# Part of the output-projection weights gathered onto 112 partitions, and the rows of o laid out to match

## The chip, the cores and the metric

The kernel runs on one core of one Trainium2 chip, with nothing beside it. Its engines are TensorE (PE; PEld is its weight load), VectorE (DVE), ScalarE (ACT), GpSimd (POOL) and SyncE (SP), and it has 16 DMA engines that fill its on-chip memory of 128 partitions from HBM. The metric is the time of one execution on the device in microseconds (us), the median of several runs. The profile is of one further execution. Its span goes from the first to the last instruction.

## The reference

One decode step, in float32: attention with a cached K and V behind a layer norm, then a two-layer perceptron behind another, both with a residual.

```python
B, Sq, D = 2, 1, 512
H, Sk, Dh = 32, 8192, 128
...
q = (x @ wq).reshape(B, Sq, H, Dh).transpose(0, 2, 1, 3)      # x behind a layer norm
scores = jnp.einsum("bhqd,bhkd->bhqk", q, k_cache) * (Dh ** -0.5)
p = softmax(scores, axis=-1)
o = jnp.einsum("bhqk,bhkd->bhqd", p, v_cache)
a = o.transpose(0, 2, 1, 3).reshape(B, Sq, H * Dh) @ wo        # wo: 4096 x 512
...
h = x + a
h2 = h + gelu(layernorm(h) @ w1 + b1) @ w2 + b2                # w1: 512 x 1792
```

K and V are 268 MB each; wq and wo have 8.4 MB each, w1 and w2 3.7 MB each.

## The kernel before

It streams K and V once. The loop runs over 64 pairs `i` of a head `h` and a batch row `b`. A pair's K is one load of 4 MB into a tile of 128 partitions x 32 KB, with 64 keys to a partition (L150 to L152), and so is its V. All of these tiles come from one pool, `kv`, of five buffers; wq before the loop, and w1 and w2 behind it, use the same pool. SP issues all these loads in the order of the program: K of pair i+1, then V of pair i-1, and it waits at each until the tile's last reader is done.

For each half of K (`c` is 0 or 1), VectorE multiplies it by q (L161), and VectorE (L170) and ScalarE (L166) sum over the head's 128 columns. The largest score of a head goes through TensorE (L180, L186), ScalarE takes the exponentials (L194), and two pairs later TensorE multiplies them with V (`values`, L215). `gather` (L222) copies that sum from PSUM. Its 32 filled rows are parts of the sum, sixteen for each batch row; `head_sum` (L232) adds them up with four products, and `head_out` scales them by the inverse of the softmax's sum (L242), so that o of the two batch rows lies in two partitions.

The projection by wo is done in groups of WG = 4 heads, so long as a head is below LG * WG = 28. `load_wo` (L55) loads a group's 512 rows of wo as four rows to a partition, 8 KB in one run, into a tile `wog` from the pool `wts` of two buffers. `head_out` writes o of the group's heads into one tile `orow` of 512 columns; `turn` (L248) transposes every fourth column into PSUM, four times, `turned` copies this to `ot4` (L252) and multiplies its four slices with the four rows (L254), which adds to `rowacc`. Heads 28 to 31 go another way: their wo has a head's 128 rows on the 128 partitions (one load for the four, L58), their o is kept on 128 partitions too, and `project` (L257) adds head by head; the last head is merged with what follows. A tile `late` for this end shares the buffers of `wog` (L338).

The group of wo is loaded at the fourth pair of its own heads, by SP, between a K load and a V load. `behind` orders what an engine does next behind a given instruction. Instruction order on an engine is otherwise that of the program, with small shifts by the scheduler. POOL does nothing but a few memsets and the identity matrix at the start.

At the end, V's last load comes in three pieces, w1 in four and w2 in six, each piece with a completion of its own. ScalarE's queue loads x at the start (L49); b1 and b2 are four small loads (L281, L282) near pair 56.

Of the kernel before, what the change touches and what calls it, by code (L numbers as in the profile page):

```python
# [8 lines left out]

F32 = mybir.dt.float32  # L10
BF16 = mybir.dt.bfloat16
AF = mybir.ActivationFunctionType
ALU = mybir.AluOpType
AX = mybir.AxisListType

P = 128
EPS = 1e-5
QG = 2
WG = 4
CH = 32  # L20
NACT = 10
BUFS = 5
# [5 lines left out]
def tile_decode_block(ctx: ExitStack, tc: tile.TileContext, x, k, v, wq, wo, w1, b1, w2, b2, out):  # L28
    nc = tc.nc
    B, H, SK, DH = k.shape  # L30
    D = x.shape[-1]
# [6 lines left out]
    SCALE = DH ** -0.5  # L38

    const = ctx.enter_context(tc.tile_pool(name="const", bufs=1))  # L40
    wts = ctx.enter_context(tc.tile_pool(name="wts", bufs=2))
    kv = ctx.enter_context(tc.tile_pool(name="kv", bufs=BUFS))
    work = ctx.enter_context(tc.tile_pool(name="work", bufs=3))
    psq = ctx.enter_context(tc.tile_pool(name="psq", bufs=2, space=bass.MemoryType.PSUM))
    psm = ctx.enter_context(tc.tile_pool(name="psm", bufs=3, space=bass.MemoryType.PSUM))
    psa = ctx.enter_context(tc.tile_pool(name="psa", bufs=1, space=bass.MemoryType.PSUM))

    x2 = const.tile([B, D], F32, name="x2")
    nc.scalar.dma_start(x2, x.rearrange("b s d -> (b s) d"))  # L49

    wo_g = {}

    LG = H // WG - 1

    def load_wo(g):  # L55
        t = wts.tile([P, WG, D], F32, name="wog")
        rows = wo[g * WG * DH:(g + 1) * WG * DH, :]
        nc.sync.dma_start(t, rows.rearrange("(h p) n -> p h n" if g == LG else "(p h) n -> p h n", p=P))  # L58
        wo_g[g] = t

    wqv = wq.rearrange("(p r) n -> p r n", r=DC)
# [1 line left out]
    for r in range(0, DC, 2):  # L63
        t = kv.tile([P, 2, H * DH], F32, name="wqs", tag="kv")
        nc.sync.dma_start(t, wqv[:, r:r + 2, :])  # L65
        wqs += [t[:, 0, :], t[:, 1, :]]

    ident = const.tile([P, P], F32, name="ident")
    make_identity(nc, ident)
    epst = const.tile([P, 1], F32, name="epst")  # L70
    nc.vector.memset(epst, EPS)
    eps2 = const.tile([P, 1], F32, name="eps2")
    nc.vector.memset(eps2, EPS * EPS)
    wb = const.tile([P, D], BF16, name="wb")
    nc.vector.memset(wb, 0.0)
# [45 lines left out]
    for r in range(DC):  # L121
        for j in range(QW // 512):
            for n in range(NG):
                nc.tensor.matmul(so2[j][32 * n:32 * n + B], yT[:, r, :],  # L124
                                 wqs[r][:, n * QW + j * 512:n * QW + (j + 1) * 512],
                                 start=(r == 0), stop=(r == DC - 1))
# [16 lines left out]
    rowacc = psa.tile([B, D], F32, name="rowacc")  # L143
    pairs = [(h, b) for h in range(H) for b in range(B)]
    NP = len(pairs)
    ST, MX, MT, GM, LT, RL, SS, OP, OT, OR, TP = {}, {}, {}, {}, {}, {}, {}, {}, {}, {}, {}

    def load(src, i, parts):
        h, b = pairs[i]
        t = kv.tile([P, NS, DH], F32, name="kv", tag="kv")  # L150
        for s0, n in parts:
            nc.sync.dma_start(t[:, s0:s0 + n], src[b, h].rearrange("(p j) d -> p j d", j=NS)[:, s0:s0 + n])  # L152
        return t
# [9 lines left out]
    def by_act(i, c, kt):  # L163
        s = ST[i]
        for j in range((c + 1) * CH - NACT, (c + 1) * CH):
            nc.scalar.activation(kt[:, j, :], kt[:, j, :], AF.Copy, accum_out=s[:, j:j + 1])  # L166
# [28 lines left out]
                                 AF.Exp, bias=nb[:, b:b + 1], scale=SCALE, accum_out=LT[h][:, b:b + 1])  # L195

    def total(h):
        if h >= LG * WG:
            RL[h] = psm.tile([P, B], F32, name="sm")
            nc.tensor.matmul(RL[h], ones, LT[h], start=True, stop=True)  # L200
        else:
            RL[h] = psm.tile([B, 1], F32, name="sm")
            nc.tensor.matmul(RL[h], LT[h], ones[:, 0:1], start=True, stop=True)  # L203

    def inverse(h):
        rl = work.tile(list(RL[h].shape), F32, name="rl" if h >= LG * WG else "rlr")
        nc.vector.reciprocal(rl, RL[h])
        RL[h] = rl

# [13 lines left out]

    def head_sum(h):
        ss = SS.pop(h)
        OP[h] = psm.tile([P, B] if h >= LG * WG else [B, DH], F32, name="sm")
        for j in range(4):
            sj = ss[:, j * DH:(j + 1) * DH]
            if h >= LG * WG:
                nc.tensor.matmul(OP[h], sj, sel[:, :, j], start=(j == 0), stop=(j == 3))  # L230
            else:
                nc.tensor.matmul(OP[h], sel[:, :, j], sj, start=(j == 0), stop=(j == 3))  # L232

    def head_out(h):
        if h >= LG * WG:
            OT[h] = work.tile([P, B], F32, name="ot")
            nc.vector.tensor_tensor(OT[h], OP.pop(h), RL.pop(h), op=ALU.mult)  # L237
        else:
            g, n = divmod(h, WG)
            if n == 0:  # L240
                OR[g] = work.tile([B, WG * DH], F32, name="orow", bufs=2)
            nc.vector.tensor_scalar(OR[g][:, n * DH:(n + 1) * DH], OP.pop(h), RL.pop(h), None, op0=ALU.mult)  # L242

    def turn(g):
        TP[g] = psm.tile([P, WG, B], F32, name="sm")
        o = OR.pop(g).rearrange("b (p r) -> b r p", r=WG)
        for r in range(WG):
            nc.tensor.transpose(TP[g][:, r, :], o[:, r, :], ident[:B, :B])  # L248

    def turned(g):  # L250
        t = work.tile([P, WG, B], F32, name="ot4")
        nc.vector.tensor_copy(t, TP.pop(g))  # L252
        for r in range(WG):
            nc.tensor.matmul(rowacc, t[:, r, :], wo_g[g][:, r, :], start=(g == 0 and r == 0), stop=False)  # L254

    def project(h):
        nc.tensor.matmul(rowacc, OT.pop(h), wo_g[LG][:, h % WG, :], start=False, stop=(h == H - 2))  # L257

    def behind(m):
        return tc.issue_after(m.ins) if m is not None else nullcontext()  # L260
# [4 lines left out]
    for i in range(NP):  # L265
        h, b = pairs[i]
        for c in range(NC):
            if c == 0:
                if i + 1 < NP:
                    kt[i + 1] = load(k, i + 1, whole if i + 1 < NP - 1 else halves)  # L270
                if i % (WG * B) == 3:
                    g = i // (WG * B)
                    if g <= LG - 1:
                        load_wo(g)
                if i == NP - 10:
                    load_wo(LG)
                if i >= 1:
                    vt[i - 1] = load(v, i - 1, whole if i < NP - 1 else halves)
                if i == NP - 8:
                    for e in range(B):  # L280
                        nc.sync.dma_start(b1r[e::32], b1.rearrange("(n f) -> n f", n=NG))  # L281
                        nc.sync.dma_start(b2s[e:e + 1], b2[None, :])  # L282
            with behind(multiply(i, c, kt[i])):
                if b == 0 and c == 0:
                    if h >= 2:
                        head_sum(h - 2)
                        head_out(h - 2)
                    if h >= 1:
                        all_max(h - 1)
                if b == 0 and c == 1 and h >= 1:  # L290
                    inverse(h - 1)
                    if h >= 2 and h % WG == 1 and h < H - 1:
                        turned(h // WG - 1)
            by_act(i, c, kt[i])
            if b == 0 and c == 0 and h >= 1:
                exps(h - 1)
            by_dve(i, c, kt[i])
            if b == 0 and c == 0:
                if h >= 1:
                    total(h - 1)  # L300
                if h >= 2 and (h - 2) // WG == LG:
                    project(h - 2)
                elif h >= 2 and (h - 2) % WG == WG - 1:
                    turn((h - 2) // WG)
            if c == 1:
                if i >= 2:
                    values(i - 2, vt.pop(i - 2))
                    if b == B - 1:
                        gather(h - 1)
                row_max(i)  # L310
                if b == 0 and h % QG == 1 and h + 1 < H:
                    make_q(h + 1)
# [10 lines left out]
    hl = H - 1  # L323
# [6 lines left out]
    inverse(hl)  # L330
    junk = const.tile([P, 2], F32, name="junk")
    nc.scalar.activation(junk[:, 0:1], LT[hl][:, 0:1], AF.Sqrt)
    wl = wo_g[LG][:, hl % WG, :]
    wsum = const.tile([P, 1], F32, name="wsum")
    nc.vector.tensor_reduce(wsum, wl, axis=AX.X, op=ALU.add)
    wmean = const.tile([P, 1], F32, name="wmean")
# [4 lines left out]
    base = late[:B, 1, :]  # L341
# [17 lines left out]
    last = values(NP - 1, vlast)  # L359
    gather(hl)  # L360
    with behind(last):
        for n in range(NG):
            last = nc.tensor.matmul(po2[32 * n:32 * n + 32], ident[:B, :32], resb[:, n * P:(n + 1) * P],
                                    start=True, stop=False)
# [10 lines left out]
    for c in range(DC):  # L375
        last = nc.tensor.matmul(acc[:, c, :], wlc.rearrange("d (p c) -> d c p", c=DC)[:, c, :], OT[hl],
                                start=True, stop=True)
    with behind(last):
        for n in range(NG):
            nc.tensor.matmul(po2[32 * n:32 * n + B], OT[hl], wl[:, n * P:(n + 1) * P],  # L380
                             start=False, stop=False)
# [8 lines left out]
    for c in range(DC):  # L390
        for n in range(NG):
            last = nc.tensor.matmul(
                pf[32 * n:32 * n + B], cen[:, c, :], w1t[:, c, n * FN:(n + 1) * FN],
                start=(c == 0), stop=(c == DC - 1))
        if c == 0:
            with behind(last):
                for n in range(NG):
                    last = nc.tensor.matmul(vp[32 * n:32 * n + 32], sv, onesd, start=True, stop=True)
# [14 lines left out]
    for t in range(FT):  # L413
        for n in range(NG):
            nc.tensor.matmul(po2[32 * n:32 * n + B], fT[:, t, :B], w2t[:, t, n * P:(n + 1) * P],
                             start=False, stop=(t == FT - 1))
# [29 lines left out]
```

## Time and profile before

| what | value |
|---|---|
| median of 3 runs | 1324.13 us (1324.02 to 1324.27) |
| the profiled execution | 1324.32 us |
| its span | 1322.5 us |
| VectorE busy | 989.5 us, 75% |
| TensorE busy | 530.4 us, 40% |
| ScalarE busy | 442.0 us, 33% |
| POOL busy | 1.3 us, 10 instructions |
| DMA | 561.64 MB, 425 GB/s over the span |
| mean granted TensorE clock | 0.664 |

A line of a group of instructions reads: source line, engine, operation, output and input tiles, shapes, count, then the busy time in us and the mean ns of one, then the idle time of the engine before them and what ended it. The stretch view gives for each stretch its length, the busy time and the number of instructions of PE, PEld, DVE, ACT and POOL, the granted clock, the mean busy share of the 16 DMA engines, and GB/s. A line of a queue has packets, MB and the share of the 16 engines' time. Beside these the trace has a record of every DMA packet (start, time, size, queue, but not its engine) and the time of each count that a DMA engine adds to a load's semaphore when its part is done; a load on all 16 engines has 16 counts.

### The profile page before, as it was taken

Reading aid. Unit: us, or ns where it says so; the run is one execution under the profiler, and the core shown is the slowest. Engines: PE = TensorE matmul, PEld = TensorE weight load, DVE = VectorE, ACT = ScalarE, POOL = GpSimd, SP = SyncE. Lnnn points to the kernel's source line nnn. Section 1 sums busy time; section 2 is a strip of 40 time slices with the busy share of each in tenths; the row PEclk is TensorE's granted clock in tenths of the full one; section 3 lists DMA queues with packets and bytes.
Section 4 is the critical chain, followed back from the end, with each engine's and each line's share of the span. In section 5 each row is a group of like instructions: output and inputs, shape, how many; then the busy total and the mean of one; then the engine's idle time right before and its main releaser. Section 6 shows DMA issues by size and latency. Waiting matters only on the chain.

```text
span 1322.5 us, 9641 instructions
## 1 busy us (share of the span) xinstructions
PE 530.4 (40%) x2901; PEld 143.3 (11%) x2901; DVE 989.5 (75%) x459; ACT 442.0 (33%) x2763; POOL 1.3 (0%) x10
## 2 busy tenths in 40 slices
PE   4044234334244244434336244263343532444347
PEld 1011001101011011100101011010011100011013
DVE  1997877867877778868778778777778768687781
ACT  0433323324323324324323333323333333243241
POOL 0000000000000000000000000000000000000000
PEclk9566666666676676676676666676766766666668
DMA  9999999999999999999999999999999999999995
GB/s 412 427 429 429 436 431 429 427 432 434 432 428 430 434 431 431 430 429 432 434 429 431 431 432 430 433 429 432 430 431 432 431 431 428 432 429 431 428 424 216
DMA packets 22364, 561.64 MB, mean 425 GB/s; under 512 B 2452, under 2 KB 2468, under 8 KB 4136
## 3 DMA queue, kind: packets, MB, share of 16 engines
q1 hardware_dynamic: 22300, 561.02, 98.9%
q8 instruction: 23, 0.38, 0.1%
q14 instruction: 29, 0.24, 0.0%
q10 hardware_dynamic: 12, 0.01, 0.0%
HBM read 561.01 MB, written 0.00 MB: 424 GB/s over the span
## 4 chain that ended last, share of the span: by engine, by line
DMA 73%; DVE 18%; PE 7%; issue 1%; ACT 0%; SPq 0%; DVEq 0%
DMA kv<-in_A_k_cache_dram 51%; DMA kv<-in_A_v_cache_dram 19%; DVE kv L161 12%; PE so L215 6%; DVE s L170 5%; DMA w1s<-in_B_w_dram 3%; DMA w2s<-in_B_w_dram 1%; PE qps L136 1%; DVE gm L184 0%; ACT kv L166 0%; DVE orow L242 0%; ACT L194 0%; DVE mx L177 0%; SPq L152 0%; SPq L65 0%
## 5 line engine op out<-in xcount | busy, mean ns | idle before, releaser
L161 DVE TENSOR_TENSOR kv<-kv,qps 128x4096 f32<-128x4096 f32 x128 | 562.3, 4413 | 286.3 <-DMA kv<-in_A_k_cache_dram 286.3
L166 ACT ACTIVATE kv<-kv 128x128 f32<-128x128 f32 x1280 | 376.0, 295 | 687.0 <-DVE kv L161 670.9
L215 PE MATMUL so<-kv,pt 128*8 128x512 f32 x2048 | 374.2, 855 | 258.6 <-DMA kv<-in_A_v_cache_dram 256.2
L170 DVE TENSOR_REDUCE s<-kv 128x22 f32<-128x2816 f32 x128 | 390.9, 3075 | 0.1
L166 ACT ACTIVATION_READ_ACCUMULATOR kv<-kv 128x1 f32 x1280 | 238.7, 187 | 0.0
L215 PEld LDWEIGHTS so<-kv,pt 128*8 128x8 f32 x2048 | 63.3, 113 | 500.2 <-DMA kv<-in_A_v_cache_dram 249.8
L186 PE MATMUL sm<-gm,srow 1*128 1x2 f32 x64 | 18.1, 349 | 192.1 <-DVE gm L184 192.1
L136 PE MATMUL qps<-q,pick 2*128 2x256 f32 x64 | 30.8, 631 | 135.7 <-DVE kv L161 135.7
L222 ACT ACTIVATE ss<-so 128x512 f32<-128x512 f32 x32 | 19.1, 597 | 148.4 <-PE so L215 148.4
L180 PE MATMUL sm<-ident,mx 128*1 128x128 f32 x64 | 17.7, 276 | 66.4 <-DVE mx L177 61.3
L254 PE MATMUL rowacc<-wog,ot 128*2 128x512 f32 x56 | 38.5, 852 | 5.2 <-DVE ot L252 5.0
L186 PEld LDWEIGHTS sm<-gm,srow 1*128 1x128 f32 x64 | 15.5, 299 | 204.2 <-DVE gm L184 160.7
L203 PE MATMUL sm<-ones,ls 128*2 128x1 f32 x56 | 5.4, 165 | 76.2 <-ACT pt L194 76.2
L232 PE MATMUL sm<-ss,sel 128*2 128x128 f32 x224 | 29.0, 273 | 13.3 <-ACT ss L222 13.1
L136 PEld LDWEIGHTS qps<-q,pick 2*128 2x128 f32 x64 | 17.5, 299 | 142.2 <-DVE kv L161 138.5
L194 ACT ACTIVATE pt<-s,nb 128x64 f32<-128x64 f32 x64 | 21.7, 340 | 1.1
L232 PEld LDWEIGHTS sm<-ss,sel 128*2 128x2 f32 x224 | 16.7, 84 | 23.5 <-ACT ss L222 19.4
L177 DVE TENSOR_REDUCE mx<-s 128x1 f32<-128x64 f32 x64 | 14.1, 220 | 6.5 <-ACT kv L166 0.2
L180 PEld LDWEIGHTS sm<-ident,mx 128*1 128x1 f32 x64 | 5.1, 79 | 122.9 <-DVE mx L177 77.0
L124 PE MATMUL so<-wqs,yT 128*2 128x512 f32 x64 | 10.8, 834 | 11.4 <-DMA wqs<-in_A_wq_dram 11.4
L184 DVE TENSOR_REDUCE gm<-sm 1x2 f32<-1x256 f32 x32 | 12.8, 401 | 0.5 <-PE sm L180 0.5
L237 DVE TENSOR_TENSOR ot<-sm,rl 128x2 f32<-128x2 f32 x4 | 0.6, 156 | 15.4 <-PE sm L230 15.4
(85 smaller groups left out, 109.6 us busy)
## 6 DMA issues: line engine op xcount, KB each, us to landing
kv<-in_A_k_cache_dram SPq DMA_DIRECT2D x63, 4096.0 KB, 42.9
kv<-in_A_v_cache_dram SPq DMA_DIRECT2D x62, 4096.0 KB, 34.4
wqs<-in_A_wq_dram SPq DMA_DIRECT2D x2, 4096.0 KB, 16.7
wog<-in_A_wo_dram SPq DMA_DIRECT2D x8, 1024.0 KB, 45.3
kv<-in_A_v_cache_dram SPq DMA_DIRECT2D x3, 2048.0 KB
kv<-in_A_k_cache_dram SPq DMA_DIRECT2D x2, 2048.0 KB, 40.1
w1s<-in_B_w_dram SPq DMA_DIRECT2D x4, 896.0 KB, 34.1
w2s<-in_B_w_dram SPq DMA_DIRECT2D x2, 1024.0 KB
```

The lines of the kernel that those rows point to most:

```text
L136: nc.tensor.matmul(t[:, b], pick[32 * n:32 * n + B, b, :], q2[32 * n:32 * n + B, at:at + QG * DH], start=True, stop=True)
L161: return nc.vector.tensor_tensor(kc, kc, qb, op=ALU.mult)
L166: nc.scalar.activation(kt[:, j, :], kt[:, j, :], AF.Copy, accum_out=s[:, j:j + 1])
L170: nc.vector.tensor_reduce(ST[i][:, a:e], kt[:, a:e, :], axis=AX.X, op=ALU.add)
L177: nc.vector.tensor_reduce(MX[h][:, b:b + 1], ST[i], axis=AX.X, op=ALU.max)
L180: nc.tensor.transpose(MT[h][:, e, :], MX[h][:, e:e + 1], ident)
L186: nc.tensor.matmul(GM[h], srow, gm, start=True, stop=True)
L194: nc.scalar.activation(ptz[h % 2][b][:, :, 4 * b:4 * b + 4], s.rearrange("p (u j) -> p u j", j=4), AF.Exp, bias=nb[:, b:b + 1], scale=SCAL ...
L215: m = nc.tensor.matmul(so[32 * n:32 * n + 4 * B], ptz[h % 2][b][:, u, :], vt[:, 4 * u:4 * u + 4, :], start=(b == 0 and u < NG), stop=(b == ...
L222: nc.scalar.activation(SS[h], so2[h % 2], AF.Copy)
L232: nc.tensor.matmul(OP[h], sel[:, :, j], sj, start=(j == 0), stop=(j == 3))
L254: nc.tensor.matmul(rowacc, t[:, r, :], wo_g[g][:, r, :], start=(g == 0 and r == 0), stop=False)
```

## The change

wo is now loaded in five parts. Heads 0 to 6 and 7 to 13 are two groups of seven heads, 896 rows each. 896 rows are eight for each of 112 partitions; partitions 0 to 7 and 32 to 39 get none. Such a group is loaded by POOL's queue in two indexed gathers (`load_spread`), each of 128 indices, one for a partition: index m names the m-th run of four rows (8 KB) of that half of the group, counted over the 112 partitions. The sixteen partitions left out have the index 65536, which is over the bound of 111 and is not moved. Their rows in the tile are set to 0 by two memsets of 8 partitions x 4096 first. The index list `at` is made once at the start by three iotas and two memsets. A group's instructions on POOL (a copy of one number of `mx` as a gate, two memsets, two gathers) are kept in order by `next_of_pool`. The first group's gate is the maximum of head 0, the second's that of head 8.

Heads 14 to 19 are a group of six rows to a partition (two of heads 14 and 15, four of heads 16 to 19), and heads 20 to 27 one of eight rows (two parts); SP loads them as before, each part with one DMA. Heads 28 to 31 have a tile of their own, `wol`, in a pool of its own. The pool `wts` has one buffer of 16 KB a partition in place of two of 8 KB; `late` shares it.

`orow` is one tile for the whole kernel, [2, 8, 128], set to 0 at the start: a row of it has o's columns in the order of the partitions that hold the matching rows of wo, with a gap at those left out. `head_out` writes a head's part in one to two pieces, cut where the gap or a run ends. `turn` and `turned` run four times, with 8, 8, 6 and 8 slices, in place of seven times with 4. The descriptor scratch of POOL's DMAs is set to 4096.

Cut to what does something (the line numbers of the new kernel are those of the profile after):

```diff
-WG = 4
+WG = 8
+LH = 4
+UH = 7
+SHUT = (0, 32)
...
-    wts = ctx.enter_context(tc.tile_pool(name="wts", bufs=2))
+    wts = ctx.enter_context(tc.tile_pool(name="wts", bufs=1))
+    wtl = ctx.enter_context(tc.tile_pool(name="wtl", bufs=1))
...
+    HL = H - LH
+    NP7 = P - 8 * len(SHUT)
+    groups = [[(0, UH, 0)], [(UH, UH, 0)], [(14, 2, 0), (16, 4, 2)], [(20, 4, 0), (24, 4, 4)]]
+    spread_groups = 2
...
     def load_wo(g):
         t = wts.tile([P, WG, D], F32, name="wog")
-        rows = wo[g * WG * DH:(g + 1) * WG * DH, :]
-        nc.sync.dma_start(t, rows.rearrange("(h p) n -> p h n" if g == LG else "(p h) n -> p h n", p=P))
+        for h0, n, r0 in groups[g]:
+            nc.sync.dma_start(t[:, r0:r0 + n], wo[h0 * DH:(h0 + n) * DH, :].rearrange("(p r) n -> p r n", r=n))
         wo_g[g] = t
...
+    orow = const.tile([B, WG, P], F32, name="orow")
+    nc.gpsimd.memset(orow, 0.0)
+    at = const.tile([P, 1], I32, name="at")
+    gate0 = const.tile([1, 1], F32, name="gate0")
+    pool = [nc.gpsimd.iota(at, [[0, 1]], base=-8, channel_multiplier=1)]
...
+    next_of_pool(lambda: nc.gpsimd.iota(at[32:64], [[0, 1]], base=16, channel_multiplier=1))
+    next_of_pool(lambda: nc.gpsimd.iota(at[64:], [[0, 1]], base=48, channel_multiplier=1))
+    for p0 in SHUT:
+        next_of_pool(lambda: nc.gpsimd.memset(at[p0:p0 + 8], 1 << 16))
+    runs = wo.rearrange("(m r) n -> m (r n)", r=4)
+
+    def load_spread(g, gate):
+        t = wts.tile([P, WG, D], F32, name="wog")
+        h0, n, _ = groups[g][0]
+        next_of_pool(lambda: nc.gpsimd.tensor_copy(gate0, gate))
+        for p0 in SHUT:
+            next_of_pool(lambda: nc.gpsimd.memset(t[p0:p0 + 8], 0.0))
+        dst = t.rearrange("p (s r) n -> p s (r n)", s=2)
+        for s in range(2):
+            next_of_pool(lambda: nc.gpsimd.indirect_dma_start(
+                dst[:, s], None, runs, bass.IndirectOffsetOnAxis(at, 0),
+                element_offset=(h0 * DH + s * NP7 * 4) * D, bounds_check=NP7 - 1, oob_is_err=False))
+        wo_g[g] = t
+
+    def load_last():
+        t = wtl.tile([P, LH, D], F32, name="wol")
+        nc.sync.dma_start(t, wo[HL * DH:, :].rearrange("(h p) n -> p h n", p=P))
+        wo_g["last"] = t
...
     def head_out(h):
...
+            while a < end:
+                if g < spread_groups:
+                    run, at = divmod(a, NP7 * R)
+                    p = at // R + 8
+                    stop = a - at + 24 * R
+                    if at >= 24 * R:
+                        p += 8
+                        stop = a - at + NP7 * R
+                    rows = slice(run * R, run * R + R)
+                else:
+                    p, stop, rows = a // R, end, slice(r0, r0 + R)
+                stop = min(stop, end)
+                cols = slice(a - (h - h0) * DH, stop - (h - h0) * DH)
+                nc.vector.tensor_scalar(orow[:, rows, p:p + (stop - a) // R].rearrange("b r p -> b p r"),
+                                        op[:, cols].rearrange("b (p r) -> b p r", r=R), rl, None, op0=ALU.mult)
+                a = stop
...
-                if i % (WG * B) == 3:
-                    g = i // (WG * B)
-                    if g <= LG - 1:
+                for g in range(spread_groups, len(groups)):
+                    if i == 2 * (groups[g][0][0] + 2):
                         load_wo(g)
...
             if c == 1:
+                for g in range(spread_groups):
+                    if i == 2 * (groups[g][0][0] + (2 if g else 1)):
+                        load_spread(g, MX[h - 1][:1, 0:1])
...
-    nc = _bacc.Bacc("TRN2", target_bir_lowering=False, num_devices=1)
+    nc = _bacc.Bacc("TRN2", target_bir_lowering=False, num_devices=1,
+                     dynamic_dma_scratch_size=4096)
```

## The prediction

> **What bounds the kernel now.** I read the page first: the DMA share, the queues, and the chain that ended last.
>
> ```profile
> DMA  9999999999999999999999999999999999999995
> q1 hardware_dynamic: 22300, 561.02, 98.9%
> q8 instruction: 23, 0.38, 0.1%
> q14 instruction: 29, 0.24, 0.0%
> ...
> DMA 73%; DVE 18%; PE 7%; issue 1%; ACT 0%; SPq 0%; DVEq 0%
> ...
> L161 DVE TENSOR_TENSOR kv<-kv,qps 128x4096 f32<-128x4096 f32 x128 | 562.3, 4413 | 286.3 <-DMA kv<-in_A_k_cache_dram 286.3
> ...
> kv<-in_A_k_cache_dram SPq DMA_DIRECT2D x63, 4096.0 KB, 42.9
> kv<-in_A_v_cache_dram SPq DMA_DIRECT2D x62, 4096.0 KB, 34.4
> wog<-in_A_wo_dram SPq DMA_DIRECT2D x8, 1024.0 KB, 45.3
> ```
>
> The 16 DMA engines are busy in every slice but the last; VectorE waits 286 us in all for K. A K load lands 42.9 us after its issue, and a load takes about 9.7 us to move, so several are always queued. Only bytes per engine, or the share of one engine, can matter. So I asked next for the stretches at the end.
>
> ```profile
> 1200.00:1240.00 40.00, 16.82 (x80) 4.28 (x80) 31.55 (x14) 14.55 (x94) 0.00 (x0) 0.59 1.00 431
> ...
> 1303.00:1308.00 5.00, 4.38 (x40) 3.38 (x40) 0.65 (x4) 0.60 (x1) 0.00 (x0) 0.89 0.84 304
> 1308.00:1309.00 1.00, 1.00 (x12) 0.23 (x8) 0.00 (x0) 0.00 (x0) 0.00 (x0) 0.50 0.12 45
> 1309.00:1318.00 9.00, 6.80 (x135) 3.15 (x127) 1.49 (x3) 2.71 (x4) 0.00 (x0) 0.93 0.06 26
> ```
>
> The last two columns are the DMA share and GB/s. From 1309 to 1318 the share is 0.06, one engine of sixteen, at 26 GB/s, about 431/16. **One engine works alone for the last 10 us**: in the packet records its row follows without a gap to 1318.2, while the other fifteen stop between 1307.6 and 1308.1.
>
> The trace also keeps the sixteen completion counts of each load. Their spread is 0.4 us for the load that lands at 42 us and grows in steps of 0.6 to 0.9 us to 15.4 us at 1252. The second latest engine is then 5.0 us behind the first, and 5.1 at the end. The steps fall where queue 14 fetches 8 KB of instructions: the packet at 47.43 takes 0.31 us and the 32 KB packet behind it 1.59 instead of 1.21, 0.68 together. Some 22 such fetches make 15 us. Queue 8's 16 KB fetches cost 1.07 + 0.50 = 1.57 us each, but are spread over the other engines.
>
> **Which engine is late.** Two small loads tell. b1r has four rows, each moved by another engine; issued at 1126.8, they run at 1149.19, 1149.21, 1153.13 and 1162.98: the last is the late engine, which carries none of b2s's one-row loads (both at 1149.3 to 1149.4, on another of the four). Followed back packet by packet, the late engine starts with the packet at 1.78 or at 1.85 us. Both end at 3.87 (3.868 and 3.867), where the next two start (3.864 and 3.866), so the order doesn't separate them. But of the sixteen second packets only two took 1.213 us, all others 1.220 or more: the late engine's at 3.864, and one at 3.799. Each has two possible forerunners, and each time one of them (at 1.78 and at 2.06) stands behind one of the two rows of x on the same engine. So I take the late engine as one of the two that moved x: in the order in which loads are split, the first two, and by b2s not the first.
>
> **The change part by part.**
>
> 1. *wo of heads 0 to 13.* The trace has 1152 packets of 8 KB on queue 1: 256 for w2, 896 for wo of 28 heads. Fourteen heads are 448, 28 on each engine. At the late engine's pace at the end (8 packets of w2 from 1309.47 to 1311.95, 0.310 each) that is 8.7 us. The gathers move the same 448 packets, 112 in each of four, from 112 partitions. A load over 128 partitions gives eight to each engine (8 packets of 32 KB on each), so sixteen partitions are two engines' worth, and fourteen engines would carry 32 packets each, 4 x 0.310 = 1.24 us more. Which partitions an engine writes no row shows. Bounds for the late engine: -8.7 us if its eight are all left out, +1.24 if none is. I take -8.7: the lowest partitions are left out, and x and b1r show the lowest rows of a load with the first engines of the split, of which the late one is one.
>
> The Trainium skill, DMA: Bandwidth & Descriptors, section The descriptor swizzle, gives the map: the first engine writes partitions 0 to 3 and 32 to 35, the second 4 to 7 and 36 to 39. By it the rows left out are just those two engines', and the sum is the -8.7 above. The same page, Rules for kernel authors, speaks against: transfers to disjoint partition halves both spread over all 16 engines, so leaving partitions out would free none, and the sum would be 0. No run here shows either yet.
>
> 2. *Balance after it.* Late engine: 15.4 - 8.7 = 6.7 us behind the old leader. Second latest: 5.1 + 1.24 = 6.3. So 0.4 us is left before another engine sets the end, and nearly every extra cost of a gather's packet would show. The trace has none; bounds: 0, from the pace of SP's own 8 KB packets, and 0.37 a packet, from the instruction fetch (0.68 for 8 KB). The latter is price by bytes, not by change of queue: 16 KB costs 1.57, more than twice as much, so no fixed part is left. A gather lands in the same buffers as SP's loads, so I take near the low end: 32 x 0.03 = 1.0 us, less 0.4 in hand: +0.6.
>
> 3. *The compute at the end.* It must move too. The last products (L415) wait little for w2: 80 of 112 ran in 2.37 us from 1314.60, so without w2 they would end at 1317.9 instead of 1319.1, 1.2 us. But K of the last pairs is itself waited for (4.95 us of idle VectorE before 1252.41), and every landing there is the late engine's, so K, V, w1 and w2 all come earlier together.
>
> 4. *SP.* Eight wo loads become five; three issues of 0.42 us go, hidden by the queue. The first that is left waits for the gathers, which landed hundreds of us before. Behind it stand V loads, with 34 us in hand.
>
> 5. *POOL.* Four memsets of 8 x 4096: by L95 (128 elements a partition in 0.204 us) at most 6.5 us each. The first gate opens with mx of head 0 at 51.5 us, and TensorE reads the group at head 8, near 344 us (the first L254 stands at 224.9 for head 5; a head is 39.8). The second is issued behind head 8 and read near 620. A gather's start cost is in no row; with over 200 us of cover I count 0. If POOL took longer than that, the projection would block V.
>
> 6. *VectorE.* Six more pieces of orow (28 to 34, L242 0.331) and three fewer copies (0.133): 1.6 us, perhaps double with the stride; one more memset is POOL's. Hidden by the 286 us of waiting. The write of late (L340) waits 2.8 us for L254 now; behind sixteen products instead of eight it waits some 6 us more (8 x 0.69, the 38.5 us of L254 by 56), and the K product behind it, which has 1.05 us to spare there, starts 4.5 us late; the next pairs idle 4.4 us each, so it is gone after one or two.
>
> 7. *TensorE.* Two more transposes (0.26) and two more rows of projection (four products of 0.69); the bursts are up to twice as long, so V's buffer comes free 5.5 us later at three heads. Cover: 34 us of queue. Without it each would delay a V load by that.
>
> Sum on the profiled execution: 1324.32 (span 1322.5 and 1.8 around it) - 8.7 + 0.6 = 1316.2; the median lies 0.2 lower: **1316.0 us**.
>
> **Rivals.**
>
> - *The gather's packets are dear.* Fourteen engines take them. With c us a packet the second latest engine ends at 5.1 - 8.7 + 32c; it passes the relieved late engine at c = 0.32 and the old end at 0.59. For it: the only packets between SP's that the trace has cost 0.68. Against: those go to an engine's instruction store, and cost by size. At 0.45 the end is 5.1 - 8.7 + 14.4 = 10.8, 4.6 us better: 1319.5. At 0.68 it is 18.2: 2.8 us **slower**, 1326.9, though the late engine is free.
> - *Another map.* If eight neighbours make one engine's share, partitions 0 to 7 and 32 to 39 are the first and fifth engine, the late one is the second and gets 1.24 us more: 1325.4. If partitions are dealt in turn, eight engines lose 2 of 8 and the late one moves 24 packets instead of 28: 1322.9.
> - *The indices beyond the bound are dropped before the split*, so that 112 rows go evenly to 16 engines: 28 packets for each, as before: 1324.1, the change doing nothing. This is also where the rule on halves would end.
>
> A change of the DMA engine that fetches, with the new program, would look like wrong engines; that no engine's instruction count changes much speaks against it.
>
> **Chances.** Relief as summed 0.70 (1314.5 to 1318.5), relief with dear packets 0.06 (to 1321.5), dealt in turn 0.03, nothing done 0.07, wrong engines 0.05, dear beyond 0.59 us a packet 0.09. The bound of 0.2% is 2.6 us, about what a measurement of this kernel can tell from no change. So faster is 0.70 + 0.06 = 0.76; within it lie dealt in turn, nothing done and wrong engines, 0.15; slower 0.09. The range runs from 1314.5 (no cost of the gathers, and 0.9 below that for chance in the fetches) to 1324.2, which takes in dealt in turn and nothing done: 0.86 by the cases, less what each case may miss. The likeliest case alone has 1314.5 to 1318.5.
>
> **What would show it.** The stretch behind the last full share: no 10 us at 0.06, but all engines stopping within about 1 us. The spread of a load's counts falls by some 4.3 us at each group's gathers, and ends near 7. 448 packets of 8 KB on POOL's queue, 0.31 to 0.34 us each. L306 34 times, TensorE's L320 60 times, no new wait of TensorE for wog. If the lone stretch is still there, and about 1.2 us longer, the map is wrong; if it is gone but the time isn't, the packets are dear.

## The result and the profile after

The changed kernel takes 1317.42 us (median of five runs, 1317.31 to 1317.44) against 1324.13 (1324.02 to 1324.27): ratio 0.9949 (95% interval 0.9935 to 0.9963), 6.7 us faster. The forecast was 1316.0. The profiled execution took 1317.44 us, its span is 1315.5.

The page of the changed kernel, in the order of the lines shown before the change: DMA share, queues, chain, the K product, the loads.

```profile
DMA  9999999999999999999999999999999999999997
q1 hardware_dynamic: 21868, 557.35, 98.8%
q0 software_dynamic: 576, 3.67, 0.7%
q8 instruction: 23, 0.38, 0.1%
q14 instruction: 29, 0.24, 0.0%
...
DMA 73%; DVE 20%; PE 6%; issue 1%; ACT 0%; SPq 0%; DVEq 0%
...
L211 DVE TENSOR_TENSOR kv<-kv,qps 128x4096 f32<-128x4096 f32 x128 | 562.2, 4413 | 274.7 <-DMA kv<-in_A_k_cache_dram 274.7
...
L107 POOL MEMSET wog<- 8x4096 f32 x4 | 14.0, 3502 | 6.0 <-PE rowacc L320 5.9
...
kv<-in_A_k_cache_dram SPq DMA_DIRECT2D x63, 4096.0 KB, 42.7
kv<-in_A_v_cache_dram SPq DMA_DIRECT2D x62, 4096.0 KB, 33.7
...
wog<-in_A_wo_dram SPq DMA_DIRECT2D x3, 1024.0 KB, 38.8
```

The kernel is bound as before. The 576 packets of queue 0 are the gathers: 448 of 8 KB and 128 of 4 bytes. Of the 128, 64 are completion counts, sixteen for each of the four gathers, and 64 fit the dropped indices, one packet for each: the run below that drops none has 64 such packets for its four gathers, and the two that drop eight a gather have 96. VectorE does the same K work and waits 11.6 us less for K. The new memsets took 14.0 us of an idle POOL. The stretches at the end (last three columns: granted clock, DMA share, GB/s):

```profile
1300.00:1303.00 3.00, 3.00 (x33) 0.90 (x36) 0.66 (x4) 0.80 (x2) 0.00 (x0) 0.51 0.96 394
1303.00:1308.00 5.00, 3.11 (x38) 0.96 (x35) 1.33 (x2) 1.91 (x3) 0.00 (x0) 0.95 0.81 322
1308.00:1312.00 4.00, 3.40 (x106) 2.15 (x96) 0.00 (x0) 0.00 (x0) 0.00 (x0) 1.00 0.36 137
1312.00:1316.00 4.00, 0.00 (x0) 0.00 (x0) 0.29 (x1) 0.00 (x0) 0.00 (x0) 0.72 0.01 1
```

The nine microseconds at 0.06 are gone: now the share falls from 0.96 through 0.81 and 0.36 to nothing. The last w2 piece lands at 1311.50 instead of 1318.68.

The sixteen completion counts of the last K load's second half (the first of them at 1256.5 before and at 1249.6 after), each in us behind the first, sorted (from the trace's counts):

```
before   0  0.3 0.3 0.4 0.5  1.7  3.0  3.1  3.1  3.4  4.2  4.7  4.7  4.9  5.0  15.4
after    0  9.4 9.4 9.6 9.8 10.7 12.3 12.5 12.6 12.8 13.6 14.2 14.3 14.3 14.4  14.9
```

One engine now leads the rest by 9.4 us, about 32 packets of 0.30 (28 that it lost and 4 that the others gained): it is emptied, and was not late. Behind it the old order is kept, except that the straggler has joined the others. The lead and the relief came in two steps, at the two groups' gathers.

### The profile page after: what moved, and what is told of

Same layout as the page of the kernel before. It is cut to its first block, busy times and chain, and to the rows that moved or that the text cites. A ratio compares the mean times of both kernels' runs of the same rounds, so it can differ in the third digit from the quotient of the medians.

```text
span 1315.5 us, 9681 instructions
## 1 busy us (share of the span) xinstructions
PE 530.3 (40%) x2906; PEld 144.4 (11%) x2907; DVE 990.2 (75%) x462; ACT 442.0 (34%) x2763; POOL 21.2 (2%) x26
## 4 chain that ended last, share of the span: by engine, by line
DMA 73%; DVE 20%; PE 6%; issue 1%; ACT 0%; SPq 0%; DVEq 0%
DMA kv<-in_A_k_cache_dram 57%; DMA kv<-in_A_v_cache_dram 12%; DVE kv L211 12%; DVE s L220 7%; PE so L265 4%; DMA w1s<-in_B_w_dram 3%; PE rowacc L320 1%; DMA w2s<-in_B_w_dram 1%; PE qps L186 0%; SPq L202 0%; DVE orow L306 0%; DVE gm L234 0%; ACT kv L216 0%; ACT L244 0%; DVE mx L227 0%
## 5 line engine op out<-in xcount | busy, mean ns | idle before, releaser
L265 PE MATMUL so<-kv,pt 128*8 128x512 f32 x2048 | 367.2, 858 | 199.6 <-DMA kv<-in_A_v_cache_dram 197.2
L107 POOL MEMSET wog<- 8x4096 f32 x4 | 14.0, 3502 | 6.0 <-PE rowacc L320 5.9
L234 DVE TENSOR_REDUCE gm<-sm 1x2 f32<-1x256 f32 x32 | 12.6, 395 | 0.5 <-PE sm L230 0.5
```

Source lines behind the costliest of these rows:

```text
L107: next_of_pool(lambda: nc.gpsimd.memset(t[p0:p0 + 8], 0.0))
L265: m = nc.tensor.matmul(so[32 * n:32 * n + 4 * B], ptz[h % 2][b][:, u, :], vt[:, 4 * u:4 * u + 4, :], start=(b == 0 and u < NG), stop=(b == ...
```

## The experiments

Times are medians in us beside the kernel before on the same chip (1324.2 each time); in brackets stand the ratio to it and its 95% interval. No run changed what is computed. Edits are shown in their main lines, against the changed kernel unless the text says otherwise; the pair at which the second group's gathers are issued moves with the groups (18, 20 or 21).

**Which rows are left out.** The first two runs keep the gathers and move the gap, or take it away; the index list and the rows of o follow OPEN, and GROWS is a group's count of wo rows.

```diff
-    NP7 = P - 8 * len(SHUT)
+    OPEN = [p for p in range(P) if p not in (*range(64, 72), *range(96, 104))]
+    GROWS = len(OPEN) * WG
...
-        for p0 in SHUT:
-            next_of_pool(lambda: nc.gpsimd.memset(t[p0:p0 + 8], 0.0))
+        for p0, n in ((64, 8), (96, 8)):
+            next_of_pool(lambda: nc.gpsimd.memset(t[p0:p0 + n], 0.0))
```

> Same gathers, same sizes, same grouping; the sixteen rows left out are 64-71 and 96-103 instead of 0-7 and 32-39. Theory 'place' (each partition belongs to a fixed DMA engine, and the late engine owns part of 0-7 and 32-39): the late engine now moves 32 of the 8 KB packets instead of 28, 4 x 0.310 = 1.24 us more: 1324.1 + 1.2 = 1325.4, with the lone stretch at a DMA share near 0.06 back and some 10 us long. Rival 'form' (the gain comes from the gathers on another queue, or from seven heads in one tile, whatever rows are left out): 1317.4 as in the changed kernel, no lone stretch.

```diff
-    NP7 = P - 8 * len(SHUT)
+    OPEN = [p for p in range(P) if p not in ()]
+    GROWS = len(OPEN) * WG
```

> wo of heads 0 to 15 by the same kind of gather, on all 128 partitions with no index beyond the bound (two groups of eight heads, four gathers of 128 packets). Theory 'place': every engine moves 32 packets of 8 KB for these heads, as before: 1324.1, up to 1325 if a gather's packet costs a few hundredths more, with the lone stretch of some 10 us back. Rival 'form': 1317 to 1318.

Measured: 1327.12 (1.0022, 1.0012 to 1.0032) and 1326.09 (1.0014, 1.0004 to 1.0024). The end of the run with 64 to 71 and 96 to 103 left out, then of the run without a gap:

```profile
1308.00:1310.00 2.00, 2.00 (x20) 1.12 (x23) 0.49 (x3) 0.00 (x0) 0.00 (x0) 0.50 0.69 245
1310.00:1318.00 8.00, 6.26 (x59) 1.51 (x55) 1.49 (x3) 2.71 (x4) 0.00 (x0) 0.71 0.10 38
1318.00:1322.00 4.00, 3.30 (x104) 2.07 (x92) 0.29 (x1) 0.00 (x0) 0.00 (x0) 1.00 0.06 20
```

```profile
1308.00:1310.00 2.00, 2.00 (x20) 1.18 (x24) 0.50 (x3) 0.00 (x0) 0.00 (x0) 0.71 0.60 190
1310.00:1318.00 8.00, 6.27 (x103) 2.62 (x99) 1.49 (x3) 2.71 (x4) 0.00 (x0) 0.86 0.07 28
```

In both the stretch with one engine at work, or little more, is back (26 GB/s is one engine's rate; 38 and 28 over the 8 us). The place of the rows decides, not the form. Without the gap the straggler is 15.4 us behind, as before; the changed kernel stands 8.67 us below that run. But both are 1.7 to 2.0 us slower than 'place' gave: something costs every kernel of this kind some time.

**Which engine.** Two groups of 7.5 heads on 120 partitions, with one engine's eight left out; `orow` has two buffers, since head 7 belongs to both groups. The mirror run has range(0, 4) and range(32, 36).

```diff
-    NP7 = P - 8 * len(SHUT)
+    OPEN = [p for p in range(P) if p not in (*range(4, 8), *range(36, 40))]
+    GROWS = len(OPEN) * WG
```

> Heads 0 to 14 and half of a group more evenly: two groups of 7.5 heads on 120 partitions, left out are only 4-7 and 36-39. Theory 'second engine' (the late engine writes 4-7 and 36-39): it loses 30 packets, 30 x 0.310 = 9.3 us, the others get 32 for 30, 0.62 more instead of 1.24 in the changed kernel: 1317.4 - 0.6 = 1316.8. Rival 'first engine' (the late one writes 0-3 and 32-35): 1324.1 + 0.6 = 1324.8 with the lone stretch back.

> The mirror of the run before: left out are only 0-3 and 32-35, heads 0 to 14 on 120 partitions. Theory 'second engine': the late engine is not relieved and gets 0.62 more: 1324.1 + 0.6 = 1324.8, lone stretch some 10 us. Rival 'first engine': 1316.8.

Measured: 1316.73 (0.9943, 0.9927 to 0.9960) and 1326.66 (1.0018, 1.0009 to 1.0028). The late engine writes 4 to 7 and 36 to 39; leaving out 0 to 3 and 32 to 35 was of no use, and without it the kernel is 0.7 us faster than the changed one. The counts of the last K load's second half are then spread over 5.5 us, with no engine far ahead and none far behind.

**Half of it.**

```diff
-    groups = [[(0, UH, 0)], [(UH, UH, 0)], ...
-    spread_groups = 2
+    groups = [[(0, UH, 0)], [(7, 4, 0), (11, 2, 4), (13, 1, 6)], ...
+    spread_groups = 1
```

> Only heads 0 to 6 by gathers with the holes; heads 7 to 13 by plain loads on all partitions (four heads, two, one). Theory 'place': the late engine loses 14 packets of 8 KB, half of the relief: measured 6.7 us for the whole group of 28, so 1324.2 - 14 x 0.310 = 1319.9 if the relief is proportional, and up to 1321.1 if the gathers carry a fixed loss of 1.2 us that half of them has too. Rival 'form': 1317.4 or 1324 (all or nothing).

Measured: 1321.56 (0.9980, 0.9971 to 0.9990), 2.6 us. If half of the 8.7 is gained, a loss of about 1.7 is left: it is there at full size and doesn't go with the number of gathers.

**The same rows by plain loads.**

```diff
-            next_of_pool(lambda: nc.gpsimd.indirect_dma_start(dst[:, s], None, runs, ...
+            for p0, p1 in ((8, 32), (40, P)):
+                m0 = h0 * DH + s * NP7 * 4 + (p0 - 8 * (1 + p0 // 32)) * 4
+                nc.sync.dma_start(t[p0:p1, 4 * s:4 * s + 4],
+                                  wo[m0:m0 + (p1 - p0) * 4, :].rearrange("(p r) n -> p r n", r=4))
```

> The changed kernel's tiles, rows of o and holes, but wo of heads 0 to 13 comes by plain loads from SP (for each gather one load of 24 partitions, 8-31, and one of 88, 40-127) instead of gathers. Theory 'place by partition' (any load to a partition is moved by the engine that owns it): the late engine is relieved by 28 packets as with the gathers: 1317.4, no lone stretch. Rival 'place by order' (a plain load is cut into sixteen shares in the order of its rows, whatever the partitions are): every engine carries about 28 of the 448 packets, 1324.1 (up to 1325 where the rows left over by sixteen fall to the first engines), lone stretch of some 10 us. On the other question: if packets are some 0.7 ns longer wherever POOL's queue is in use (1218.78 ns for 32 KB before, 1219.5 to 1219.8 in the five kernels with gathers), the mean here is 1218.8; if the grouping or the rows of o cause it, 1219.5 or more.

Measured: 1351.90 (1.0214, 1.0197 to 1.0231), its four times lying between 1349.75 and 1353.85; both theories fell. Stretches of this run, the first two around the two groups' loads, the last near its end:

```profile
67.00:101.00 34.00, 16.17 (x83) 5.11 (x83) 25.10 (x12) 11.91 (x67) 0.00 (x0) 0.69 1.00 310
455.00:500.00 45.00, 10.43 (x64) 2.57 (x54) 18.52 (x11) 7.48 (x46) 0.00 (x0) 0.65 1.01 339
1335.00:1342.00 7.00, 5.10 (x87) 2.33 (x83) 1.33 (x2) 1.50 (x3) 0.00 (x0) 0.84 0.06 26
```

All sixteen engines are busy, but move 310 and 339 GB/s instead of 431: (431 - 310) / 431 x 34 + (431 - 339) / 431 x 45 = 19.2 us of the 25.6 by which this profiled execution (1349.75) lies above 1324.2. The rest is not traced. In the packet records mostly ten to twelve 8 KB packets are under way at a time in these loads, beside some five of other sizes, and each takes 0.72 and 0.63 us (medians of the two groups) instead of 0.31. The lone engine is still there at the end. The Trainium skill, DMA: Bandwidth & Descriptors, section Why a DMA increments its semaphore by 16 and not by 1, says that a load uses the largest number of engines up to 16 that divides its count of partitions, and the lowest-numbered ones: eleven for 88, twelve for 24, the late engine among them. The ten to twelve in the trace agree. Why their packets took twice as long stays open.

**The loss that all share.** In the packet records a 32 KB packet took 1218.78 ns on the mean before, and 1219.47 to 1219.80 in the kernels with gathers. That is about 0.9 ns on each of an engine's 1016 such packets, 0.9 us. The first suspect was POOL's queue. The next edit adds one tiny gather to the kernel before, with the tiles and the scratch that it needs.

```diff
+    at = const.tile([P, 1], I32, name="at")
+    nc.gpsimd.iota(at, [[0, 1]], base=0, channel_multiplier=1)
+    few = const.tile([P, 8], F32, name="few")
+    nc.gpsimd.indirect_dma_start(few, None, x.rearrange("b s (c e) -> (b s c) e", e=8),
+                                 bass.IndirectOffsetOnAxis(at, 0), bounds_check=P - 1, oob_is_err=False)
...
+                     dynamic_dma_scratch_size=4096)
```

> The kernel before, with one gather of 128 indices of 32 bytes each on POOL at the start, whose data nobody reads, and nothing else changed. Theory 'queue' (once POOL's queue is in use, each later packet of SP's queue takes 0.7 to 1.0 ns longer, 1016 packets of 32 KB on each engine): mean of a 32 KB packet 1219.5 to 1219.8 ns, time 1324.2 + 1.0 = 1325.2 (up to 1326). Rival 'form of the change' (the loss comes from the gathers' own packets, the grouping or the rows of o): 1218.8 ns and 1324.2 (within 0.3).

> The kernel before, profiled once more. If the mean of a 32 KB packet differs from one execution to the next, it is anywhere in 1218.5 to 1220 ns; if it belongs to the kernel, 1218.8 again within 0.2 ns, and w1's last piece lands at 1305.7 on the late engine.

Measured: 1325.70 (1.0011, 1.0001 to 1.0021) with a mean packet of 1219.70 ns, and 1218.64 ns for the kernel before profiled again. So the pace belongs to the kernel, and this little edit brings the loss. The queue seemed to be it; but in the changed kernel the packets were longer ahead of the first gather already. The plain loads speak against the queue too: that run has no gather, and between 42 and 60 us, ahead of its first 8 KB packet, its 32 KB packets took 1219.32 ns (before: 1216.84). The next two edits are of the run with the tiny gather; one takes the gather out, the other moves it.

```diff
-    nc.gpsimd.indirect_dma_start(few, ...)
+    nc.gpsimd.memset(few, 0.0)
```

> The run with the tiny gather, which cost 1.5 us, with the gather itself taken out: its two tiles, its index list and the 4096 bytes of scratch for POOL's transfers stay. Theory 'queue' (a program that uses POOL's queue has longer packets): 1324.2 and 1218.7 ns for a mean 32 KB packet. Rival 'layout' (the scratch and the two tiles move the other tiles in memory, and that makes the packets longer): 1325.7 and 1219.7 ns. For the rival: in the changed kernel the packets between 42 and 60 us are already at 1219.35 ns (before 1216.84), though the first gather starts at 63.9.

```diff
-    nc.gpsimd.indirect_dma_start(few, ...)
+    gate0 = const.tile([1, 1], F32, name="gate0")
...
+                if i == 40:
+                    m = nc.gpsimd.tensor_copy(gate0, MX[h - 1][:1, 0:1])
+                    with tc.issue_after(m.ins):
+                        nc.gpsimd.indirect_dma_start(few, ...)
```

> The same tiny gather, but issued behind the 21st head's first scores, at some 420 us of the span or later, instead of at the start. If a gather lengthens the packets that come after it, those before it take 1218.2 ns and those after 1219.2, and the time is 1324.2 + 1.5 x 0.65 = 1325.2. If it is enough that the program has the queue (or if it is the layout), all packets from 42 us on are at 1219.2 to 1219.4 ns and the time is 1325.7.

Measured: 1325.61 (1.0011, 1.0001 to 1.0020) without any gather, so 'queue' fell; and 1316.85 (0.9944, 0.9927 to 0.9961) with the gather late, which no theory had: 7.4 us **faster** than before, with all of wo on the old path. Its mean 32 KB packet is 1214.70 ns, and the packets are this short from the first K on, though the gather's own ran at 789 us. What it has and the two runs before it don't is the tile `gate0`, 32 bytes, ahead of the buffers. The compiled programs give the addresses of the K and V buffers within a partition; over a multiple of 512 bytes they begin at

```
160   before                                        1218.78, again 1218.64 ns   1324.2 us
224   changed kernel, every other run up to here    1219.5 to 1219.8 ns
256   tiny gather late                              1214.70 ns                  1316.85 us
```

(the plain loads, also at 224, apart: their own packets disturb the mean). The last two runs change the length of one tile. That moves the buffers of K, V and wo, with every other tile behind it, and changes nothing else: 120 in the changed kernel takes them from 224 to 160, and 16 in the kernel that leaves out 4 to 7 and 36 to 39 takes them from 224 to 256.

```diff
-    gate0 = const.tile([1, 1], F32, name="gate0")
+    gate0 = const.tile([1, 120], F32, name="gate0")
```

> The changed kernel with one tile of 32 bytes made 480 bytes long and nothing else, so that the K and V buffers and wo's tiles begin 448 bytes further on: at 160 over a multiple of 512 bytes of their partition, as in the kernel before, instead of 224. Theory 'layout' (the changed kernel lost time because its buffers stand at other addresses): mean 32 KB packet back to 1218.7 ns and the time 1317.4 - 1.4 = 1316.0. Rival 'gather' (the loss is the price of the gathers): 1219.5 ns and 1317.4.

> The run that leaves out 4-7 and 36-39 alone (1316.7, mean 32 KB packet 1219.71), with the same tile 64 bytes long instead of 32, which puts K, V and wo's tiles at multiples of 64 bytes, as they stand in the run with the tiny gather late. Theory 'layout': 1214.7 ns, 1016 x 5.0 ns = 5.1 us, and 0.7 to 1.0 more from shorter fetches and 8 KB packets: 1310.6 (1309 to 1312). Rival 'the late gather' (what made that run fast is when its gather ran, or another thing in it): 1316.7 and 1219.7 ns.

Measured: 1316.19 (0.9940, 0.9923 to 0.9957) with 1218.54 ns, and 1309.71 (0.9891, 0.9874 to 0.9907) with 1214.61 ns. 'Layout' holds in both. The second is the best version found, 14.5 us below the kernel before and 7.7 below the changed one. Its end:

```profile
1295.00:1300.00 5.00, 3.40 (x22) 0.66 (x15) 1.08 (x2) 1.56 (x3) 0.00 (x0) 0.78 0.94 387
1300.00:1303.00 3.00, 2.70 (x96) 2.27 (x96) 0.25 (x1) 0.00 (x0) 0.00 (x0) 1.00 0.57 228
1303.00:1308.00 5.00, 1.04 (x28) 0.21 (x16) 0.29 (x1) 0.00 (x0) 0.00 (x0) 0.95 0.05 16
```

## Why the prediction was right, and where it was not

The kernel got faster for the reason given, and the time lies in the range, 1.4 us above the forecast.

- *Bound, and which engine is late (step 1): right, shown.* The engine of 4 to 7 and 36 to 39 is the straggler, the second of the split, as taken from x, b1r and b2s. The -8.7 is the difference between the changed kernel and gathers of the same kind without the gap, -8.67. The map of the Trainium skill, DMA: Bandwidth & Descriptors, section The descriptor swizzle, agrees (one engine for exactly these eight). The page's rule on partition halves, from which the prediction drew that nothing would be freed, does not carry over to these gathers, whose sixteen dropped indices freed two engines.
- *Balance and the price of a gather's packet (step 2): the size about right, by luck; the reason not.* The +0.6 stood for 0.03 us more a packet. The gathers' packets took 0.317 us, SP's 8 KB packets in the same run 0.318. What 512 gathered packets, with their grouping and rows of o, add at like addresses is the run without a gap against the one without gathers, 1326.09 - 1325.61 = 0.5 us in all, whose place is open. The balance itself was right: against the four engines that fetched least (9.4 to 9.8), the last ended 5.3 us behind and the next 4.8. The forecast's 6.7 and 6.3, counted from before the gathers, are 5.5 and 5.1 less the 1.24 that those four carry too.
- *The step that failed is the sum: it had no term for the addresses.* The edit puts 64 bytes more ahead of the K and V buffers, and each of an engine's 1016 packets of 32 KB takes some 0.7 ns longer (1219.49 on the mean against 1218.78). With the buffers back at 160 (1218.54 ns) the same kernel takes 1316.19, 0.2 from the forecast: the term is 1.2 us here, and 1.4 between the run without gathers and the kernel before. The 32 KB packets account for 0.9 to 1.0 us of it, the rest is not traced. -8.7 + 0.5 + 1.4 = -6.8; measured -6.7.
- *The end (step 3): right.* The last K that VectorE waits for lands 7.4 us earlier (1252.38 to 1244.94), w2's last piece 7.2.
- *SP, POOL, VectorE, TensorE (steps 4 to 7): hidden, as counted.* POOL's memsets took 3.5 us each under a bound of 6.5; TensorE never waits for wo; the write of `late` waits 6.2 us (8.8 forecast), and VectorE idles again for K from the next pair on (1.5 us, then 3.8). The view of groups, by shape, has the rows of o in 34 pieces:

```profile
L306 DVE TENSOR_SCALAR orow<-sm,rlr 2x128 f32<-2x128 f32 x22 | 9.2, 418 | 0.0
L306 DVE TENSOR_SCALAR orow<-sm,rlr 2x96 f32<-2x96 f32 x4 | 1.4, 362 | 0.0
L306 DVE TENSOR_SCALAR orow<-sm,rlr 2x32 f32<-2x32 f32 x4 | 1.0, 252 | 0.0
L306 DVE TENSOR_SCALAR orow<-sm,rlr 2x64 f32<-2x64 f32 x4 | 1.0, 307 | 0.0
```

  12.6 us instead of 28 x 0.331 = 9.3, and no idle time in front.
- *What would show it: half right.* The lone stretch is gone, but the spread of the counts ends at 14.9, not near 7, and on w2's last piece the fifteen engines behind the first stop up to 5.4 us apart, where about 1 us was forecast. The forecast forgot that the first engine, emptied without having been late, would now lead; leaving it in its share is what the better version does. The 5.4 us are the spread that the fifteen have among themselves on the last K already (5.5); before the change the fifteen ahead of the straggler were 5.0 us apart there and 0.6 on w2's last piece.
- *Rivals.* Dear packets are refuted by the 0.317 us, another map and dropping before the split by the runs that moved, halved or removed the gap.

## What to carry to other kernels

Where one DMA engine is last and the others wait for it, an indexed gather that leaves out just that engine's partitions takes work from it, and no more should be left out than that; a plain load of fewer partitions is no substitute. Where the DMA engines bound a kernel, look at the addresses of the streamed buffers before and after every edit that adds or drops a tile: a control at the same addresses is needed before a microsecond is put down to the edit itself. Here 32 bytes were worth 7.0 us (1316.73 to 1309.71), more than the change.

## What the runs showed of the hardware

- A mean 32 KB packet into buffers that begin at a multiple of 256 bytes takes 1214.6 to 1214.7 ns (two kernels); 160 bytes over one 1218.5 to 1218.8 (two kernels), 224 over one 1219.5 to 1219.8 (eight kernels). On 1016 packets an engine that is 4 to 5 us. The Trainium skill, DMA: Bandwidth & Descriptors, section How a descriptor splits into AXI transactions, says of reads that a start off a 256-byte boundary costs the beats of 32 bytes in front of it; five and seven on 1024 would be an estimated 0.5% and 0.7%, the traces show 0.3% and 0.4% for the buffers that are written. Whether 64 bytes are enough no run tells: both runs are at a multiple of 256. Why the address counts stays open.
- Fetches get cheaper too: queue 8's 16 KB packets took 1070 ns on the mean in the run without gathers (224) and 944 with the tiny gather late (256), and the straggler was 12.8 us behind instead of 15.2. With 5.0 us of 32 KB packets that makes up most of the 8.8 us between the two.
